# 24 token tiles transposed through DRAM and VectorE's 32x32 block transpose

## The chip, the core and the metric

The program runs on one core of a Trainium2 chip. Its engines work in parallel, each through its own list of instructions in order, and wait for each other by semaphores: TensorE (PE: matrix products and transposes; PEld: its weight loads), VectorE (DVE), ScalarE (ACT), GpSimd (POOL) and SyncE (SP), which here only issues transfers. SBUF has 128 partitions; PSUM takes the results of TensorE. The metric is the device time of one execution in microseconds, as the median of several runs.

## The reference

Two layers, each of FNet mixing and a linear attention block, on x of 2048 tokens by 640 columns, 32 heads of 20:

```
def _A_ref(x, dft_seq_re, dft_seq_im, dft_hid_re, dft_hid_im):
    a = jnp.einsum("bsd,ed->bse", x, dft_hid_re)
    b = jnp.einsum("bsd,ed->bse", x, dft_hid_im)
    return jnp.einsum("ts,bse->bte", dft_seq_re, a) - jnp.einsum("ts,bse->bte", dft_seq_im, b)

def _B_ref(x, wqkv, wo):
    qkv = (x @ wqkv).reshape(B, S, 3, H, Dh).transpose(2, 0, 3, 1, 4)
    q, k, v = qkv[0], qkv[1], qkv[2]
    phi = lambda t: jnp.where(t > 0, t + 1, jnp.exp(t)) + 1e-6
    pq, pk = phi(q), phi(k)
    kv = jnp.einsum("bhsd,bhse->bhde", pk, v)
    z = jnp.einsum("bhsd->bhd", pk)
    num = jnp.einsum("bhqd,bhde->bhqe", pq, kv)
    den = jnp.einsum("bhqd,bhd->bhq", pq, z)[..., None] + 1e-6
    return (num / den).transpose(0, 2, 1, 3).reshape(B, S, D) @ wo

for layer in range(2):
    x = x + _A_ref(_layernorm(x), dft_seq_re, dft_seq_im, dft_hid_re, dft_hid_im)
    x = x + _B_ref(_layernorm(x), wqkv, wo)
```

The change lies in `_B_ref`: in how the normalised x becomes an operand of the products for q and k.

## The kernel before

**Tiles and products.** The tokens lie in 16 tiles of 128 rows. A product of a tile with a 640x640 weight goes over five chunks of 128 columns of the tile, and each chunk must stand transposed in SBUF, its columns on the partitions. Single precision is made of two parts of a shorter type: hi, a rounded copy, and lo, the rest (`split`: the copy on ScalarE at L122, the subtraction at L123, on VectorE). `product` (L156) issues for each chunk hi·hi, hi·lo and lo·hi, each in two halves of 320 columns: 30 matmuls for a product.

**The first passes.** `keys_values` holds the place of the change. Its first loop (L282 on) runs over ten tiles, n = 0 to 9; a stage of Gram products (L244) follows, then the loop runs over the other six tiles, then a second Gram stage. That happens in both layers. An iteration for tile n does this, in the program's order:

- the statistics and the norm of tile n+1 (L116, x to t);
- the key product of tile n, and `phi` on its result: two steps from PSUM on ScalarE (L276, L277), an exp on ScalarE (L278), and one step on VectorE (L279), which gives s;
- POOL adds s to a running sum (L292);
- `chunks`: five transposes of tile n+1 on TensorE (L128) into PSUM, then hi from PSUM on ScalarE (L122) and lo, PSUM minus hi, on VectorE (L123);
- the query product of tile n, and the same `phi`, which gives pq;
- after some tiles, two further pieces of work. After tiles 4, 5, 8, 13 and 15 of the first layer SyncE saves two tiles of weights to DRAM (L199), from where the second layer loads them again. After the tiles 1, 2, 4, 5, 6, 7, 10, 11 and 12 in both layers there is a check: the program takes mirror symmetries of the DFT matrices for granted, and looks at them piece by piece on VectorE (L1071, L1088: ck, junk, cm), and falls back to a general path if they don't hold. Each check ends by issuing the loads of the next pieces (L1063) on SyncE, into the four buffers of the pool `raw`.

The transposes stand before the query product in TensorE's list, and the products of tile n+1 can start only with hi and lo.

**What sets the order.** A scheduler orders the instructions of TensorE, VectorE, ScalarE and POOL here, by priorities that follow the program's order, moved by a table of offsets (`AHEAD`, read by `ahead`), and by times of its own. SyncE keeps the program's order. Tiles come from pools: 12 buffers for the temporaries t (`tmp`), 31 for w and s (`wp`), 16 for pq, 4 for ck and raw weights, and four tiles of PSUM.

Of the kernel before, what the change touches and what calls it, by code (L numbers as in the profile page):

```python
# [8 lines left out]
F32 = mybir.dt.float32  # L9
# [5 lines left out]
S, D, H, DH = 2048, 640, 32, 20  # L15
NT = S // 128
ND = D // 128
# [17 lines left out]
SECOND = 'x02d x12d x22d x32d x00d x01d x10d x11d W00d W01d W02d W10d | w00a | w01a v00v W11d | w02a v01v W12d | v02v | R0a V0a w10a | O0p sfa v10v ffv dfp kfa r3p | w11a c2v v11v w12a nfa v12v nea t2p a3v b3v c3v V1a t3p p1v m1p u20v u21v u23v u24v u22v'  # L35
KM = (0, 0)
LEAD = 3
LOADS = (13, 13, 15, 15)
# [10 lines left out]
class K:  # L49
# [82 lines left out]

    def split_chunks(self, tp):
        hi, lo = self.temp(F32R), self.temp(F32R)
        self.split(tp[:, :D], hi, lo)
        return [[t[:, 128 * c : 128 * c + 128] for c in range(ND)] for t in (hi, lo)]
# [24 lines left out]
class Attention:  # L161
    def __init__(self, k, X, order, order2, wqkv, wo, mask, saved=None):
        self.k, self.X, self.order, self.order2, self.mask, self.saved = k, X, order, order2, mask, saved
        self.wqkv, self.wo, self.W = wqkv, wo, {}
        self.kept = {}

    def wt(self):
# [33 lines left out]
    def normed(self, n):  # L201
        xn = self.k.temp()
        x = self.X[self.order[n]]
        with self.k.ahead("stats", n):
            self.kept[n] = self.k.stats(
                x, xn if n in ASTATS[self.k.layer] else None, True, self.k.nc.vector if n in VSTATS[self.k.layer] else None
            )
        with self.k.ahead("norm", n):
            self.k.norm(x, xn, self.kept[n])
        return xn  # L210
# [45 lines left out]
    def keys_values(self, check=None, keep=1, saves=()):  # L256

        saves = list(saves)
        k, nc, W = self.k, self.k.nc, self.W
# [20 lines left out]

        x, acc, tail = self.x0, [], None
        for a, b in ((0, CUT), (CUT, NT)):  # L282
            pks = []
            for n in range(a, b):
                with k.ahead("normed", n + 1):
                    xn = self.normed(n + 1) if n + 1 < NT else None
                pk = self.slot()
# [5 lines left out]
                pks.append(pk)  # L293
                def chunks(xn=xn, n=n):
                    tp = k.transposed(xn)
                    with k.ahead("chunks", n):
                        return k.split_chunks(tp)
# [22 lines left out]
                if xn is not None:  # L320
                    x = got[0]
            G = [k.psum() for _ in range(3)]
            tail = tail or k.psum()
# [11 lines left out]
            if a == 0:  # L335
                acc = [self.slot() for _ in range(ND)]
# [8 lines left out]
        c = ND - 1  # L345
# [780 lines left out]
def fast_path(k, ctx, x, wqkv, wo, mask, sign, cls, cex, hid, ckc, ckh, out):  # L1126
# [6 lines left out]
    X = []  # L1133
    for i in range(NT):
        t = xp.tile([128, D], F32, name=f"x{i}")
# [54 lines left out]

    dram = ctx.enter_context(k.tc.tile_pool(name="dram", bufs=1, space=bass.MemoryType.DRAM))
    saved = {
# [3 lines left out]
    for layer in range(2):  # L1196
        att = Attention(k, X, order, list(range(NT)), wqkv, wo, mask, saved if layer else None)
        k.part = 2 * layer
        four.run(T, att)
        att.keys_values(check, saves=() if layer else [(*key, v) for key, v in saved.items()])  # L1200
        k.layer, k.part = 1, 2 * layer + 1
        T = Fold(k, X)
        if layer == 0:
            with k.tc.manual_schedule(engines=three):
                steps = T.script(SECOND, four)
                att.outputs_by_hand(T, steps)
                for _ in steps:
                    pass
        else:
            k.ends, flags = check.ends, []  # L1210
            att.outputs(store, lambda: flags or flags.append(verdict(k)))
# [174 lines left out]
```

## Time and profile before

| what | value |
| --- | --- |
| median of three runs | 768.3 us (767.63 to 768.64) |
| the profiled execution | 769.53 us, of which the span is 767.7 us |
| granted TensorE clock, mean of the span | 0.999 |
| first passes, layer 1: products L156 from, to | 79.0 to 172.9, and 217.0 to 268.3 us |
| first passes, layer 2: last product ends, and the second part | 540.0, and 583.9 to 635.1 us |
| Gram stages L244 between and behind them | 172.8 to 217.2, 268.1 to 296.6, 539.9 to 584.0, 634.9 to 663.2 us |
| TensorE busy, 66 to 165 us of the span | 97.83 of 99.00 us |
| TensorE busy, 165 to 240 us | 75.00 of 75.00 us |
| DMA share, 66 to 165 us | 0.44, at 133 GB/s |

The span runs from the first to the last instruction; the execution's own time is 1.8 us more. In the profile's rows the columns of the timeline are start, duration, engine, line, operation, the tile written and those read, and behind "<-" in brackets the idle time before it with what ended it. In the chain of waits a row has the start, the time, the engine, the tile and the line. A group's row has the busy time, the mean of one in ns, then the idle time before them and its releaser. In the view of one line or tile stand the least, the median and the highest duration in ns.

### The profile page before, as it was taken

The numbers are of one execution on the slowest core, as the hardware profiler recorded it, in microseconds if no ns is written. First come the engines' busy times: TensorE is split into PE (matmuls) and PEld (weight loads), VectorE is DVE, ScalarE is ACT, GpSimd is POOL, SyncE is SP. The second block draws the span as 40 slices with busy tenths as digits, with TensorE's granted clock in tenths as the row PEclk, the third lists the DMA queues.
The fourth block names the chain that finished last, engine by engine and source line by source line (L and its number), as shares of the span: only waits on it lengthen the run. The fifth ranks groups of instructions, "written<-read, shape, count | busy, mean of one in ns | idle before, by whom it ended". The sixth has DMA issues, their size and how long they took to land.

```text
span 767.7 us, 12873 instructions
## 1 busy us (share of the span) xinstructions
PE 742.9 (97%) x4884; PEld 706.1 (92%) x4884; DVE 572.8 (75%) x1152; ACT 340.5 (44%) x642; POOL 254.7 (33%) x267
## 2 busy tenths in 40 slices
PE   4899999999999999999999999999999999999996
PEld 1388999999999999899977999999999999989996
DVE  6998875767767585988974896576766867599982
ACT  7745444455334543455682234445432455331110
POOL 5237931220121111467762693111000111243300
PEclk9999999999999999999999999999999999999999
DMA  9322333653354641500052222254224404001112
GB/s 326 101 81 87 92 100 116 189 179 98 119 148 148 215 144 24 150 7 1 14 192 70 69 92 74 75 150 147 59 91 148 134 15 151 22 12 68 70 70 73
DMA packets 35102, 79.15 MB, mean 103 GB/s; under 512 B 4276, under 2 KB 6071, under 8 KB 35031
## 3 DMA queue, kind: packets, MB, share of 16 engines
q1 hardware_dynamic: 35031, 78.23, 32.1%
q8 instruction: 41, 0.67, 0.4%
q14 instruction: 30, 0.25, 0.1%
HBM read 66.01 MB, written 11.80 MB: 101 GB/s over the span
## 4 chain that ended last, share of the span: by engine, by line
PE 76%; DVE 12%; ACT 5%; POOL 2%; DMA 2%; issue 2%; SPq 1%; DVEq 0%; ACTq 0%; POOLq 0%
PE ps L156 47%; PE ps L244 17%; PE ps L128 3%; PE ps L1013 3%; PE ps L959 2%; PE ps L396 2%; PE ps L918 1%; DVE w L123 1%; DVE t L123 1%; ACT ab L779 1%; DMA x<-in_x 1%; DVE ps L458 1%; DVE x L484 1%; ACT ab L780 1%; DVE t L462 1%
## 5 line engine op out<-in xcount | busy, mean ns | idle before, releaser
L156 PE MATMUL ps<-w,t 128*128 128x320 f32 x2880 | 439.1, 311 | 0.5 <-DVE w L123 0.2
L156 PEld LDWEIGHTS ps<-w,t 128*128 128x128 f32 x2880 | 423.0, 188 | 1.6 <-DVE t L123 0.8
L292 POOL TENSOR_TENSOR t<-t,s 128x640 f32<-128x640 f32 x32 | 57.3, 1789 | 257.7 <-DVE s L279 250.1
L244 PE MATMUL ps<-t,t 128*128 128x256 f32 (+1 forms) x640 | 139.8, 309 | 0.0
L276 ACT ACTIVATE t<-ps 128x640 f32<-128x640 f32 x64 | 45.2, 706 | 154.2 <-PE ps L156 154.2
L244 PEld LDWEIGHTS ps<-t,t 128*128 128x128 f32 x640 | 107.3, 188 | 0.0
L1088 DVE CUSTOM_DVE_ANT_0 junk<-ck,ck 128x688 bf16<-128x688 f32 (+5 forms) x138 | 99.0, 718 | 6.1 <-DMA ck<-in_ck 4.2
L244 PE MATMUL ps<-w,t 128*128 128x384 f32 (+1 forms) x320 | 98.8, 310 | 0.3 <-DVE w L123 0.3
L442 POOL TENSOR_TENSOR t<-pq,t 128x640 f32<-128x640 f32 x32 | 53.7, 1684 | 95.9 <-ACT t L365 46.5
L122 ACT CAST t<-ps 128x640 fp32r<-128x640 f32 (+1 forms) x66 | 45.8, 695 | 78.9 <-PE ps L128 73.7
L123 DVE TENSOR_TENSOR t<-ps,t 128x640 fp32r<-128x640 f32 (+1 forms) x66 | 53.9, 818 | 26.5 <-ACT t L122 25.6
L279 DVE SCALAR_TENSOR_TENSOR pq<-t,pq 128x640 f32<-128x640 f32 x32 | 26.7, 835 | 52.2 <-ACT t L278 52.2
L244 PEld LDWEIGHTS ps<-w,t 128*128 128x128 f32 x320 | 60.1, 188 | 0.7 <-DVE w L123 0.5
L959 PE MATMUL ps<-t,u 128*128 128x322 f32 x306 | 48.8, 316 | 1.4 <-ACT t L986 0.7
L959 PEld LDWEIGHTS ps<-t,u 128*128 128x128 f32 x306 | 45.9, 189 | 3.2 <-issue 0.9
L278 ACT ACTIVATE t<-t 128x640 f32<-128x640 f32 x64 | 48.0, 751 | 0.0
L123 DVE TENSOR_TENSOR t<-t,t 128x640 fp32r<-128x640 f32 x32 | 27.8, 867 | 26.5 <-ACT t L122 26.1
L128 PE MATMUL ps<-ident,t 128*128 128x128 f32 x320 | 45.5, 273 | 1.0 <-DVE t L468 1.0
L116 DVE TENSOR_SCALAR t<-x,kept 128x640 f32<-128x640 f32 x60 | 43.4, 724 | 4.0 <-PE ps L244 4.0
L128 PEld LDWEIGHTS ps<-ident,t 128*128 128x128 f32 x320 | 38.3, 140 | 2.4 <-POOL t L442 1.0
L122 ACT CAST t<-t 128x640 fp32r<-128x640 f32 x32 | 23.3, 728 | 38.3 <-DVE t L116 33.6
L1013 PE MATMUL ps<-cw,ab 128*128 128x512 f32 x80 | 35.4, 596 | 2.0 <-ACT t L743 0.9
(180 smaller groups left out, 875.9 us busy)
## 6 DMA issues: line engine op xcount, KB each, us to landing
ck<-in_ck SPq DMA_DIRECT2D x48, 346.0 KB
ck<-in_ck SPq DMA_DIRECT2D x48, 344.0 KB
save<-w SPq DMA_DIRECT2D x20, 320.0 KB
w<-save SPq DMA_DIRECT2D x20, 320.0 KB
x<-in_x SPq DMA_DIRECT2D x16, 320.0 KB
out<-x SPq DMA_DIRECT2D x15, 320.0 KB
raw<-in_wqkv SPq DMA_DIRECT2D x10, 320.0 KB
s<-in_wqkv SPq DMA_DIRECT2D x10, 320.0 KB
```

The costliest lines, as they stand in the source:

```text
L122: self.nc.scalar.copy(hi, src)
L123: self.engine(pool).tensor_tensor(lo, src, hi.bitcast(F32), op=ALU.subtract)
L128: self.nc.tensor.transpose(tp[:, 128 * c : 128 * c + 128], src[:, 128 * c : 128 * c + 128], self.ident)
L156: nc.tensor.matmul(pu[:m, 512 * h : 512 * h + HD], s, w[:, HD * h : HD * h + HD], start=first, stop=last)
L244: nc.tensor.matmul(self.place(G, c, part), x[:, 128 * c : 128 * c + 128], p[:, f : f + n], start=start and i == 0, stop=stop and i == 2, s ...
L276: nc.scalar.activation(h2(e), halves(pu), AF.Relu, scale=-1.0)
L278: nc.scalar.activation(e, e, AF.Exp, scale=-1.0)
L292: nc.gpsimd.tensor_tensor(pksum, pksum, pk, op=ALU.add)
L442: k.nc.gpsimd.tensor_tensor(t1, self.PQ[self.order2[n]], self.zb, op=ALU.mult)
L959: self.k.nc.tensor.matmul(po[:, o : o + 322], s[:, f : f + 128], w[:, x, :], start=start, stop=stop)
L1013: self.k.nc.tensor.matmul(self.sum(j), T.out["o", q][:, 128 * j : 128 * j + 128], self.C[2, g], start=n == 0, stop=n == 3)
L1088: i = nc.vector.tensor_tensor_reduce(k.junk[:, : a.shape[1]], b, a, 1.0, 0.0, op0, op1, o)
```

## The change

Tiles 4 to 15 of each layer (`TURNED`), 24 in all, get their transposed chunks another way. The norm of such a tile is made three tiles ahead (`LEADS`) and stored by a transfer to a new tile in DRAM (`turn_out`, L139 of the changed kernel). Two tiles ahead a load brings it back (`turn_in`, L144), so that the four blocks of 160 columns come to lie on four groups of 32 partitions. VectorE's transpose of 32x32 blocks (`turned`, L148 and L149) then gives the chunks in SBUF; it writes every fourth column. hi and lo (L125, L126) are made from that tile, not from PSUM. Which column of x is on which partition of which chunk differs from before: the rows of the weights for q and k are put in that order on the host, and the tiles that TensorE still transposes (0 to 3) get it by their norm, which writes pieces of 32 columns (`chunked`). The general path keeps its old way.

```diff
@@ -34,6 +34,9 @@
...
 KM = (0, 0)
+TURNED = (tuple(range(4, 16)), tuple(range(4, 16)))
+TLOWS = ((), ())
+LEADS = (3, 2)
 LEAD = 3
 LOADS = (13, 13, 15, 15)
 ASTATS = ((11,), (1,))
@@ -130,9 +133,27 @@
             )
         return tp
 
-    def split_chunks(self, tp):
+    def turn_out(self, xn):
+
+        src = self.dram.tile([4, 128, D // 4], F32, name=self.nm("turn"))
+        self.nc.sync.dma_start(src.rearrange("a p c -> p a c"), xn.rearrange("p (a c) -> p a c", a=4))
+        return src
+
+    def turn_in(self, src):
+        z = self.temp()
+        self.nc.sync.dma_start(z, src.rearrange("a (j t) c -> (a j) (t c)", t=4))
+        return z
+
+    def turned(self, z, pool):
+        t = self.temp()
+        self.nc.vector.transpose(
+            t.rearrange("p (b j t) -> p t b j", b=ND, t=4), z.rearrange("p (t b i) -> p t b i", t=4, b=ND)
+        )
+        return self.split_chunks(t, pool)
+
+    def split_chunks(self, tp, pool=0):
         hi, lo = self.temp(F32R), self.temp(F32R)
-        self.split(tp[:, :D], hi, lo)
+        self.split(tp[:, :D], hi, lo, pool)
         return [[t[:, 128 * c : 128 * c + 128] for c in range(ND)] for t in (hi, lo)]
 
 
@@ -163,6 +184,7 @@
         self.k, self.X, self.order, self.order2, self.mask, self.saved = k, X, order, order2, mask, saved
         self.wqkv, self.wo, self.W = wqkv, wo, {}
         self.kept = {}
+        self.turns, self.tlows = (TURNED[k.layer], TLOWS[k.layer]) if saved is not None else ((), ())
 
     def wt(self):
         return self.k.wp.tile([128, 640], F32R, tag="w", name=self.k.nm("w"))
@@ -206,7 +228,11 @@
                 x, xn if n in ASTATS[self.k.layer] else None, True, self.k.nc.vector if n in VSTATS[self.k.layer] else None
             )
         with self.k.ahead("norm", n):
-            self.k.norm(x, xn, self.kept[n])
+            if n in self.turns:
+                self.k.norm(x, xn, self.kept[n])
+                return self.k.turn_out(xn)
+            chunked = xn.rearrange("p (b a i) -> p a b i", b=ND, a=4)
+            self.k.norm(x.rearrange("p (a b i) -> p a b i", a=4, b=ND), chunked, self.kept[n])
         return xn
 
     def begin(self):
@@ -278,12 +304,19 @@
             nc.scalar.activation(e, e, AF.Exp, scale=-1.0)
             nc.vector.scalar_tensor_tensor(out, e, 1e-6, out, op0=ALU.add, op1=ALU.add)
 
-        x, acc, tail = self.x0, [], None
+        x, acc, tail, out = self.x0, [], None, {}
         for a, b in ((0, CUT), (CUT, NT)):
             pks = []
             for n in range(a, b):
-                with k.ahead("normed", n + 1):
-                    xn = self.normed(n + 1) if n + 1 < NT else None
+                xn = None
+                for m in range(n + 1, n + 1 + LEADS[0]) if n == 0 else (n + 1, n + LEADS[0]):
+                    if m < NT and m not in out and (m == n + 1 or m in self.turns):
+                        with k.ahead("normed", m):
+                            out[m] = self.normed(m)
+                for m in range(n + 1, n + 1 + LEADS[1]) if n == 0 else (n + LEADS[1],):
+                    if m < NT and m in self.turns:
+                        out[m] = k.turn_in(out[m])
+                xn = out.get(n + 1)
                 pk = self.slot()
                 pu = proj(1, x)
                 with k.ahead("key", n):
@@ -292,6 +325,9 @@
                     nc.gpsimd.tensor_tensor(pksum, pksum, pk, op=ALU.add)
                 pks.append(pk)
                 def chunks(xn=xn, n=n):
+                    if n + 1 in self.turns:
+                        with k.ahead("chunks", n):
+                            return k.turned(xn, n + 1 in self.tlows)
                     tp = k.transposed(xn)
                     with k.ahead("chunks", n):
                         return k.split_chunks(tp)
@@ -1188,13 +1224,13 @@
     def store(i, a, b):
         nc.sync.dma_start(out[128 * i : 128 * i + 128, HD * a : HD * b], X[i][:, HD * a : HD * b])
 
-    dram = ctx.enter_context(k.tc.tile_pool(name="dram", bufs=1, space=bass.MemoryType.DRAM))
+    k.dram = dram = ctx.enter_context(k.tc.tile_pool(name="dram", bufs=1, space=bass.MemoryType.DRAM))
     saved = {
         (part, c): [dram.tile([128, D], F32, name=k.nm("save")) for _ in range(2)]
         for part in (1, 0) for c in range(ND)
     }
     for layer in range(2):
-        att = Attention(k, X, order, list(range(NT)), wqkv, wo, mask, saved if layer else None)
+        att = Attention(k, X, order, list(range(NT)), wqkv, wo, mask, saved if layer else {})
         k.part = 2 * layer
         four.run(T, att)
         att.keys_values(check, saves=() if layer else [(*key, v) for key, v in saved.items()])
@@ -1285,6 +1321,7 @@
     base, quad = quads()
     ps = quad.reshape(-1)
     pd = np.concatenate([np.arange(HC), np.arange(D - 1, HD, -1)])
+    turned = np.arange(D).reshape(4, ND, 32).transpose(1, 0, 2).reshape(-1)
     mask = as32(np.kron(np.eye(EC // DH, dtype=np.float32), np.ones((DH, DH), np.float32)))
     even = np.concatenate([quad[0, 0], quad[1, 0], quad[0, 1], quad[1, 1]])
     odd = np.concatenate([quad[2, 0], quad[3, 0], quad[2, 1], quad[3, 1]])
@@ -1350,7 +1387,7 @@
     ghid = lambda c: as32(c[pd][:, pd].T.reshape(ND, 128, D).transpose(1, 0, 2))
     ins = {
         "x": as32(A_x[0][ps][:, pd]),
-        "wqkv": as32(B_wqkv[pd]),
+        "wqkv": as32(np.concatenate([B_wqkv[pd][turned, : 2 * D], B_wqkv[pd][:, 2 * D :]], 1)),
         "wo": as32(B_wo[:, pd]),
         "mask": mask,
         "sign": as32(np.stack([2.0 * (np.arange(128) % 2) - 1.0, 1.0 - 2.0 * (np.arange(128) % 2)], 1).astype(np.float32)),
```

Where the order moves: VectorE, in an iteration with a check in the first layer. Here t_1465 is lo, s_1420 and pq_1468 are the results of `phi`, t_1521 is the norm of a later tile, and the rows with junk and cm are the check. Before:

```order
L1088 ISA junk,cm<-ck_1202,ck_1200 128x692
L1088 ISA cm 128x1
L1088 ISA junk,cm<-ck_1196,ck_1202 128x519
L1088 ISA cm 128x1
L123 TENSOR_TENSOR t_1465<-ps_1458,t_1464 128x640
L1088 ISA junk,cm<-ck_1196,ck_1202 128x173
L1088 ISA cm 128x1
L279 SCALAR_TENSOR_TENSOR s_1420<-t_1452,s_1420 128x640
L116 TENSOR_SCALAR t_1521<-x_128,kept_1522 128x640
L279 SCALAR_TENSOR_TENSOR pq_1468<-t_1500,pq_1468 128x640
```

The changed kernel at such a place; t_1448 is what the load brought, t_1599 its transpose, t_1602 lo, t_1656 the norm of the tile three ahead:

```order
L1124 ISA junk,cm<-ck_1432,ck_1434 128x692
L1124 ISA cm 128x1
L1124 ISA junk,cm<-ck_1434,ck_1428 128x519
L1124 ISA cm 128x1
L1124 ISA junk,cm<-ck_1434,ck_1428 128x173
L1124 ISA cm 128x1
L149 STREAM_TRANSPOSE t_1599<-t_1448 128x4x160
L305 SCALAR_TENSOR_TENSOR s_1561<-t_1593,s_1561 128x640
L126 TENSOR_TENSOR t_1602<-t_1599,t_1601 128x640
L119 TENSOR_SCALAR t_1656<-x_104,kept_1657 128x640
L305 SCALAR_TENSOR_TENSOR pq_1605<-t_1637,pq_1605 128x640
```

The block transpose stands behind the whole check and ahead of s; lo has moved from amid the check to behind s; the norm, still ahead of pq, is now of a tile two further on.

TensorE, from the end of one product to the next, before: the key product (ps_1532, weights w_675 and on), the transposes, then the query product (ps_1580, w_715 and on). t_1464 is hi, t_1465 lo.

```order
L156 MATMUL ps_1532<-w_699,t_1464 128x320 x2
L156 MATMUL ps_1532<-w_700,t_1464 128x320 x2
L156 MATMUL ps_1532<-w_699,t_1465 128x320 x2
L128 MATMUL ps_1569<-ident,t_1521 128x128 x5
L156 MATMUL ps_1580<-w_715,t_1464 128x320 x2
L156 MATMUL ps_1580<-w_716,t_1464 128x320 x2
```

In the changed kernel, where the query product of one tile (ps_1495) ends and the next tile (hi t_1490, lo t_1491) begins:

```order
L177 MATMUL ps_1495<-w_740,t_1379 128x320 x2
L177 MATMUL ps_1495<-w_739,t_1380 128x320 x2
L177 MATMUL ps_1562<-w_675,t_1490 128x320 x2
L177 MATMUL ps_1562<-w_676,t_1490 128x320 x2
L177 MATMUL ps_1606<-w_715,t_1490 128x320 x2
L177 MATMUL ps_1606<-w_716,t_1490 128x320 x2
L177 MATMUL ps_1562<-w_675,t_1491 128x320 x2
L177 MATMUL ps_1562<-w_681,t_1490 128x320 x2
```

The transposes are gone from between the products, and the first matmul that reads lo has four matmuls of the key product and four of the query product on hi ahead of it.

SyncE's list, an iteration with a check and a save, before; in_ck is the check's input:

```order
L199 DMA save_469<-w_676 128x640
L1063 DMA ck_1402<-in_ck 128x692
L1063 DMA ck_1404<-in_ck 128x692
L1063 DMA ck_1406<-in_ck 128x692
L1063 DMA ck_1408<-in_ck 128x692
L199 DMA save_470<-w_681 128x640
L199 DMA save_471<-w_682 128x640
```

In the changed kernel; turn_1335 was stored one tile earlier than turn_1446:

```order
L1099 DMA ck_1428<-in_ck 128x692
L1099 DMA ck_1430<-in_ck 128x692
L1099 DMA ck_1432<-in_ck 128x692
L1099 DMA ck_1434<-in_ck 128x692
L139 DMA turn_1446<-t_1436 128x4x160
L144 DMA t_1448<-turn_1335 128x640
L221 DMA save_470<-w_681 128x640
L221 DMA save_471<-w_682 128x640
```

A store and a load stand between the loads of the check and the saves of the next iteration.

## The prediction

> **What bounds the kernel now.** I read the page's busy shares first, then its chain of waits, then the table of windows for the first passes, which is where the change acts.
>
> ```profile
> PE 742.9 (97%) x4884; PEld 706.1 (92%) x4884; DVE 572.8 (75%) x1152; ACT 340.5 (44%) x642; POOL 254.7 (33%) x267
> PE 76%; DVE 12%; ACT 5%; POOL 2%; DMA 2%; issue 2%; SPq 1%; DVEq 0%; ACTq 0%; POOLq 0%
> ```
>
> TensorE is busy 97% of the span and holds 76% of the chain. An average doesn't say what one stage is worth, so I cut out iterations of the first pass: two of the first layer, then one of the second.
>
> ```profile
> core 0: us, PE busy (x) PEld busy (x) DVE busy (x) ACT busy (x) POOL busy (x), PEclk, DMA share, GB/s
> 149.85:159.20 9.35, 9.35 (x67) 9.35 (x67) 6.60 (x16) 4.44 (x8) 1.82 (x1) 1.00 0.48 152
> 159.20:168.55 9.35, 9.35 (x67) 9.34 (x67) 6.54 (x13) 5.69 (x10) 1.82 (x1) 1.00 0.88 283
> 607.61:616.96 9.35, 9.35 (x68) 9.35 (x67) 8.50 (x20) 4.45 (x8) 1.71 (x1) 1.00 0.50 152
> ```
>
> TensorE never idles there, at the full clock. VectorE has 2.75 us free of 9.35 in most iterations, but only 0.85 in the third row. The next rows, from the chain and from the timeline, say what the transposes cost TensorE.
>
> ```profile
> 149.85 8.80 PE ps L156 x60
> 159.20 8.80 PE ps L156 x60
> 158.49 0.71 PE L128 MATMUL ps<-ident,t 128*128 128x128 f32 x5
> ```
>
> One iteration is 60 products, 8.80 us on the chain, and five transposes. The period is 159.20 - 149.85 = 9.35, so a tile's transposes are worth 0.55 (their 0.71 overlaps the neighbours).
>
> **What goes.** Four tiles in each layer keep their transposes; 24 lose them: 24 x 0.55 = 13.2 us, the most that this can bring, if nothing else becomes late.
>
> **What is added on VectorE.** The built order moves the work of an iteration as shown above: the whole check now stands ahead of the block transpose, then s, then the low half, then the norm. I price this from one iteration with a check.
>
> ```profile
> 156.25 0.82 DVE L279 SCALAR_TENSOR_TENSOR pq<-t,pq 128x640 f32<-128x640 f32 x1 [2.64 <-ACT t L278]
> 156.99 0.33 DVE L1071 TENSOR_REDUCE ca<-ck 128x1 f32<-128x173 f32 x1
> ...
> 160.62 0.82 DVE L123 TENSOR_TENSOR t<-ps,t 128x640 fp32r<-128x640 f32 x1
> 161.36 0.33 DVE L1088 CUSTOM_DVE_ANT_0 junk<-ck,ck 128x173 bf16<-128x173 f32 x1
> ...
> 161.61 0.82 DVE L279 SCALAR_TENSOR_TENSOR s<-t,s 128x640 f32<-128x640 f32 x1
> 154.29 0.71 ACT L276 ACTIVATE t<-ps 128x640 f32<-128x640 f32 x1 [2.43 <-PE ps L156]
> 155.48 0.74 ACT L278 ACTIVATE t<-t 128x640 f32<-128x640 f32 x1
> 158.69 0.71 ACT L276 ACTIVATE t<-ps 128x640 f32<-128x640 f32 x1 [2.47 <-PE ps L156]
> 175.67 0.61 DVE L116 TENSOR_SCALAR t<-x,kept 128x640 f32<-128x640 f32 x1
> 176.37 0.73 ACT L122 CAST t<-t 128x640 fp32r<-128x640 f32 x1 [0.22 <-DVE t L116]
> ```
>
> Starts are 0.74 apart for the 0.82 us operations. The check takes 156.99 to 160.62 and 161.36 to 161.61, 3.88 us. pq stands idle for 2.64 us behind the norm until ScalarE's exp is done (155.48 + 0.74), and starts 0.03 later. A high half taken from SBUF starts 0.09 after VectorE's result (175.67 + 0.61 to 176.37) and takes 0.73.
>
> The block transpose itself is in no row. From below: the norm, also 128x640 with one input, 0.59 us. From above: half rate. A row of 320 columns takes 0.476, one of 640 takes 0.82, so 1.08 ns a column; two slots for each of 640 columns is 0.13 + 1.38 = 1.51 us.
>
> ```profile
> L116 DVE TENSOR_SCALAR t<-x,kept x60: 592/608/1858, 66.0 to 647.9; 128x640 f32<-128x640 f32 x60
> L96 DVE BATCH_NORM_STATS2 st<-x 128x6 f32<-128x320 f32 x30 | 14.1, 476 | 0.2 <-POOL x L991 0.2
> L123 DVE TENSOR_TENSOR u<-ps,u 128x512 fp32r<-128x512 f32 x12 | 8.0, 672 | 1.5 <-ACT u L122 1.5
> L942 DVE TENSOR_TENSOR u<-ps,u 128x512 fp32r<-128x512 f32 x10 | 6.6, 688 | 4.8 <-ACT u L941 4.5
> ```
>
> Its output goes to every fourth column. The two last rows are the nearest: L123 there writes every second column and takes no longer than L942, which writes them in a row. So I take the plain 0.82.
>
> Now the deadlines, counted from ScalarE's first step on a query product (154.29). pq starts 1.96 later, the check at 2.70, the block transpose at 6.58, done at 7.40; with 0.09, 0.73 and 0.03 the high half is there at 8.25. TensorE wants it after 60 products, 8.80, less the 0.20 by which ScalarE trails TensorE (158.49 to 158.69): 8.60, so 0.35 is to spare. The low half ends at 9.1; the new TensorE order runs four key and four query products on the high half first, so it isn't wanted before 8.60 + 8 x 0.147 = 9.77. Without a check the transpose runs 3.9 us earlier. Nothing is late.
>
> VectorE's own loop is closer. The low half now reads two SBUF tiles, and POOL's sum (L292) starts 0.14 us after s.
>
> ```profile
> 638.35 0.82 DVE L279 SCALAR_TENSOR_TENSOR s<-t,s 128x640 f32<-128x640 f32 x1
> 639.09 0.82 DVE L123 TENSOR_TENSOR w<-s,t 128x640 fp32r<-128x640 f32 x1
> 639.31 2.01 POOL L292 TENSOR_TENSOR t<-t,s 128x640 f32<-128x640 f32 x1 [8.10 <-DVE s L279]
> 639.82 2.18 DVE L123 TENSOR_TENSOR t<-t,t 128x640 fp32r<-128x640 f32 x1
> 601.82 1.71 POOL L292 TENSOR_TENSOR t<-t,s 128x640 f32<-128x640 f32 x1 [7.96 <-DVE s L279]
> 602.02 1.86 DVE L116 TENSOR_SCALAR t<-x,kept 128x640 f32<-128x640 f32 x1
> L123 DVE TENSOR_TENSOR t<-ps,t x66: 770/820/826, 72.9 to 753.8; 128x640 fp32r<-128x640 f32 x64, 40x640 fp32r<-40x640 f32 x2
> L123 DVE TENSOR_TENSOR t<-t,t x32: 817/826/2183, 165.6 to 650.7; 128x640 fp32r<-128x640 f32 x32
> ```
>
> Here an operation that starts behind s keeps its 0.82 and POOL waits; the next one with two SBUF inputs then stands until POOL is done (2.18). The norm does too, 1.86. With one input in PSUM, as the low half has before, none of 66 exceeds 0.83. In the new order the low half follows s, and the norm pays: it ends 0.35 after POOL (603.88 against 603.53), POOL 2.15 after s. The loop of a check iteration is then pq 0.74, check 3.88, transpose 0.74, s 0.82, and 2.43 to the next free slot (2.15 + 0.36 - 0.08): 8.61, under 8.80. The spare 0.19 is the cover: a transpose above 1.0 us ends it.
>
> In two iterations of the second layer the check has two pieces (the third row of windows).
>
> ```profile
> 596.05 0.51 DVE L1071 TENSOR_REDUCE ca<-ck 128x1 f32<-128x344 f32 x1
> 600.85 0.82 DVE L279 SCALAR_TENSOR_TENSOR s<-t,s 128x640 f32<-128x640 f32 x1
> ```
>
> From 596.05 to the norm at 602.02, less the low half and s within it (0.74 each), is 4.49. The loop is 9.22, so each loses 0.42: 0.85 together.
>
> **What is added elsewhere.** The high half from SBUF costs ScalarE 0.03 more a tile, at 44% busy: nothing, since the next query's first step comes later. The norms of the other eight tiles write pieces of 32 columns: nothing while they have the idle 2.64 ahead of pq. 48 more DMAs stand on SP's queue; behind them wait the loads of the checks and the saves of weights.
>
> ```profile
> 159.07 3.46 SPq L1063 DMA_DIRECT2D ck<-in_ck  x4
> 162.58 2.75 SPq L199 DMA_DIRECT2D save<-w  x4
> 5.63 7.17 DMA x<-in_x
> 68.99 5.00 DMA raw<-in_wqkv
> ck<-in_ck SPq DMA_DIRECT2D x48, 346.0 KB
> save<-w SPq DMA_DIRECT2D x20, 320.0 KB
> ```
>
> The four check loads go out as the check frees their buffers; then the store, whose norm was long done; then a load of an earlier store. At about 0.4 us an issue this load leaves 1.3 us after a check ends. Its transpose has its turn right after the next check, 8.80 later: 7.5 us to land. Loads of 320 KB, the size of this one, land in 5.00, and in 7.17 where all of x is under way. So it is hidden, without much room. The price if not is below.
>
> **Sum.** 13.2 - 0.85 = 12.3 us. The profiled execution took 769.5 (span 767.7) and would take 757.2; the runs' median is 768.3, 1.2 lower, and goes to **756.0**.
>
> **Rivals.** (1) *The block transpose runs at half rate*, 1.51. Then the loop of a check iteration is 9.29, against 9.35 before: only the 8 tiles without a check gain in full (4.4), the 14 with a single check gain 0.06 each (0.8), the two double ones take 9.91, 0.56 more than before (-1.1). About 4.1 us: 764.2. For it: every write lands 16 bytes from the last; against it: no stride of 8 bytes cost anything. [...]
>
> (2) *The low half loses SBUF to POOL.* In a check iteration it starts 0.85 us after the transpose ends (0.09 + 0.73 + 0.03), POOL at 0.88 (s ends at 0.82 - 0.08, and 0.14): a margin of 0.03. A loss costs 2.18 - 0.82 = 1.36, and TensorE's stall gives the next iteration that much room, so every second of 16 pays: 10.9. 766.9, no measurable change. [...]
>
> (3) *Slower: the load through DRAM lands late* and holds VectorE's queue at the transpose, with s, the low half, the norm and pq behind it, so TensorE waits for the next tile. Price: landing time less 7.5, in every second of 16 iterations (the stall gives the next load its time). A gain of 12.3 is used up at 9.0 us. For it: in 159.20 to 168.55 the queues already run at 0.88, and an iteration with check (4 x 346 KB), two saves (2 x 320) and a turned tile (its store and load, 2 x 320) moves 2.66 MB, 9.4 us at that row's 283 GB/s. 1.9 x 8 = 15: 771. Against it: the load stands ahead of its iteration's saves, and most iterations have none.
>
> **Chances.** The forecast 62%, with 754.5 to 758.5 as its own range (0.55 a tile kept, up to 0.15 lost in each check iteration); half rate 17%; POOL first 7%; late load 14%. A range of 754.0 to 767.0 leaves out the late load and little else. A difference under 0.2% (1.5 us) can't be told from none. Faster by more: the first two and a little of the third, 80%; within: 6%; slower: 14%.
>
> **What would show it.** A period of 8.80 between key products in the first passes, with no idle time of TensorE behind the low or high half, shows the main term. A mean near 0.82 for the transpose shows its price; 1.5 and a period near 9.3 beside checks show rival 1. Low halves of 2.2 us show rival 2. Idle time of VectorE ended by a DMA ahead of the block transpose shows rival 3. The forecast is wrong if the transpose takes over 1.0 us, or if the second passes or the later stages, which I take as unmoved, lengthen.

## The result and the profile after

The changed kernel takes 769.5 us (median of 8 runs, 768.82 to 770.67), the kernel before 768.2 beside it (8 runs, 767.62 to 769.59): a ratio of 1.0018, interval 1.0007 to 1.0029. The predicted time was 756.0. TensorE's transposes are gone as planned, 120 fewer, and nothing came of it. One of the four timed runs of e11_all, below, took 916.4 us at a mean granted clock of 0.753; its median and ratio are those of the other three. The page of the changed kernel, busy shares and chain:

```profile
PE 736.0 (96%) x4764; PEld 694.4 (90%) x4764; DVE 628.5 (82%) x1176; ACT 341.8 (45%) x642; POOL 261.7 (34%) x267
PE 51%; DVE 28%; ACT 8%; issue 6%; POOL 3%; DMA 3%; SPq 0%; DVEq 0%; POOLq 0%; ACTq 0%
```

TensorE's share of the chain fell from 76% to 51%, VectorE's rose from 12% to 28%, and VectorE is busy 55.7 us longer. Three iterations of the first passes, in the columns of the windows before; the cuts lie at ScalarE's first steps on query products, the first two in the first layer, the third in the second:

```profile
133.23:142.53 9.30, 9.06 (x60) 8.80 (x60) 9.15 (x16) 4.48 (x7) 2.28 (x1) 1.00 0.90 290
142.53:151.96 9.43, 9.07 (x60) 8.81 (x60) 9.14 (x16) 4.48 (x9) 2.27 (x1) 1.00 0.73 223
611.71:620.96 9.25, 9.11 (x62) 9.11 (x63) 8.06 (x19) 4.46 (x9) 2.75 (x2) 1.00 0.52 168
```

The period is 9.30 and 9.43 us where 9.35 stood before and 8.80 was forecast. VectorE is busy 9.15 of 9.30. One iteration with a check, from the timeline:

```profile
126.34 0.82 DVE L305 SCALAR_TENSOR_TENSOR pq<-t,pq 128x640 f32<-128x640 f32 x1 [0.47 <-ACT t L304]
127.08 0.32 DVE L1107 TENSOR_REDUCE ca<-ck 128x1 f32<-128x173 f32 x1
...
131.09 1.34 DVE L149 STREAM_TRANSPOSE t<-t 128x640 f32<-128x640 f32 x1
132.28 0.81 DVE L305 SCALAR_TENSOR_TENSOR s<-t,s 128x640 f32<-128x640 f32 x1
132.46 0.73 ACT L125 CAST t<-t 128x640 fp32r<-128x640 f32 x1 [1.17 <-DVE t L149]
133.22 0.83 DVE L126 TENSOR_TENSOR t<-t,t 128x640 fp32r<-128x640 f32 x1
133.23 2.29 POOL L325 TENSOR_TENSOR t<-t,s 128x640 f32<-128x640 f32 x1 [7.71 <-DVE s L305]
133.97 1.90 DVE L119 TENSOR_SCALAR t<-x,kept 128x640 f32<-128x640 f32 x1
135.78 0.81 DVE L305 SCALAR_TENSOR_TENSOR pq<-t,pq 128x640 f32<-128x640 f32 x1
```

Read it as a loop without a gap: pq 0.74, the check 4.01 (127.08 to 131.09), the block transpose 1.19 to the next start, s 0.94, the low half 0.75, the norm 1.81: 135.78 - 126.34 = 9.44. The high half (132.46) can start only behind the block transpose, so it ends at 133.19, and TensorE waits for it. What TensorE and VectorE waited for, from the table of waits (us in total, times, longest):

```profile
PEld ps L177 <- ACT t L125: 10.1, 15, 2.0
PEld ps L177 <- DVE t L126: 4.6, 6, 1.1
PE ps L177 <- ACT t L125: 5.8, 9, 1.8
PE ps L177 <- DVE t L126: 3.0, 6, 0.8
DVE t L149 <- DMA t<-turn: 6.0, 3, 2.1
```

The first four are the high and the low half. The gaps of over 0.28 us between the starts of neighbouring matmuls in the first passes, each less the usual 0.147 (8.80 us for 60), come to 11.2 us of stalls (before: 0.3).

One place costs most, at the end of the first pass of the first layer:

```profile
156.64 2.38 POOL L106 TENSOR_TENSOR kept<-ve,mhalf 128x1 f32<-128x1 f32 x3
158.37 0.61 DVE L115 TENSOR_SCALAR t<-x,kept 128x640 f32<-128x640 f32 x1 [0.96 <-POOL kept L106]
...
162.87 1.58 POOL L325 TENSOR_TENSOR t<-t,s 128x640 f32<-128x640 f32 x1 [2.67 <-DVE s L305]
162.93 2.21 DVE L126 TENSOR_TENSOR t<-t,t 128x640 fp32r<-128x640 f32 x1
162.95 1.44 PE L177 MATMUL ps<-w,t 128*128 128x320 f32 x8 [1.77 <-ACT t L125]
...
165.19 9.30 PE L177 MATMUL ps<-w,t 128*128 128x320 f32 x52 [0.81 <-DVE t L126]
```

The norm of tile 11 stands amid the check here and waits 0.96 us for POOL; the block transpose is late by that; the low half starts 0.06 behind POOL's sum and takes 2.21. TensorE stands for 1.77 and 0.81 us, and its next 52 matmuls take 9.30 us, where 52 x 0.147 is 7.64. The windows show why:

```profile
165.20:168.00 2.80, 2.80 (x10) 2.80 (x11) 2.32 (x4) 1.35 (x2) 0.00 (x0) 0.50 1.06 391
168.00:171.00 3.00, 3.00 (x21) 3.00 (x21) 2.29 (x3) 0.28 (x1) 0.00 (x0) 0.94 0.82 234
```

The granted clock was 0.50 at first: ten matmuls started 0.267 us after the one before and one 0.43, which is 1.5 us more than at 0.147. The rest of the row's surplus is the last matmul's own length (the 2880 of L177 take 0.31 us in the mean).

### The profile page after: what moved, and what is told of

The parts are those of the page before. It is cut to its first block, busy times and chain, and to the rows that moved or that the text cites. A ratio compares the mean times of both kernels' runs of the same rounds, so it can differ in the third digit from the quotient of the medians.

```text
span 767.6 us, 12773 instructions
## 1 busy us (share of the span) xinstructions
PE 736.0 (96%) x4764; PEld 694.4 (90%) x4764; DVE 628.5 (82%) x1176; ACT 341.8 (45%) x642; POOL 261.7 (34%) x267
## 4 chain that ended last, share of the span: by engine, by line
PE 51%; DVE 28%; ACT 8%; issue 6%; POOL 3%; DMA 3%; SPq 0%; DVEq 0%; POOLq 0%; ACTq 0%
PE ps L177 24%; PE ps L270 16%; DVE junk L1124 6%; PE ps L1049 4%; PE ps L995 3%; DVE t L126 3%; DVE t L149 2%; DVE t L119 2%; DVE w L126 2%; ACT t L125 2%; PE ps L131 1%; PE ps L954 1%; DVE pq L305 1%; DMA ck<-in_ck 1%; DVE st L99 1%
## 5 line engine op out<-in xcount | busy, mean ns | idle before, releaser
L177 PE MATMUL ps<-w,t 128*128 128x320 f32 x2880 | 438.9, 311 | 8.8 <-ACT t L125 5.8
L177 PEld LDWEIGHTS ps<-w,t 128*128 128x128 f32 x2880 | 424.1, 189 | 14.5 <-ACT t L125 10.1
L325 POOL TENSOR_TENSOR t<-t,s 128x640 f32<-128x640 f32 x32 | 64.6, 2018 | 284.7 <-DVE s L305 284.7
L302 ACT ACTIVATE t<-ps 128x640 f32<-128x640 f32 x64 | 45.1, 705 | 125.1 <-PE ps L177 119.5
L126 DVE TENSOR_TENSOR t<-t,t 128x640 fp32r<-128x640 f32 x56 | 50.2, 896 | 26.9 <-PE ps L270 16.1
L125 ACT CAST t<-t 128x640 fp32r<-128x640 f32 x56 | 40.8, 728 | 53.6 <-DVE t L119 26.5
L125 ACT CAST t<-ps 128x640 fp32r<-128x640 f32 (+1 forms) x42 | 28.9, 691 | 78.9 <-PE ps L131 77.9
L119 DVE TENSOR_SCALAR t<-x,kept 128x640 f32<-128x640 f32 x60 | 62.7, 1050 | 0.6 <-DMA turn<-t 0.6
L126 DVE TENSOR_TENSOR t<-ps,t 128x640 fp32r<-128x640 f32 (+1 forms) x42 | 34.1, 815 | 5.8 <-ACT t L125 4.8
L305 DVE SCALAR_TENSOR_TENSOR pq<-t,pq 128x640 f32<-128x640 f32 x32 | 27.2, 852 | 13.3 <-ACT t L304 13.3
L149 DVE STREAM_TRANSPOSE t<-t 128x640 f32<-128x640 f32 x24 | 32.1, 1339 | 6.0 <-DMA t<-turn 6.0
L125 ACT CAST t<-s 128x640 fp32r<-128x640 f32 x32 | 23.2, 725 | 29.4 <-PE ps L270 29.4
```

Of the source, the lines that this page charges most:

```text
L119: self.nc.vector.tensor_scalar(out, x, m, rs, op0=ALU.subtract, op1=ALU.mult)
L125: self.nc.scalar.copy(hi, src)
L126: self.engine(pool).tensor_tensor(lo, src, hi.bitcast(F32), op=ALU.subtract)
L149: self.nc.vector.transpose(t.rearrange("p (b j t) -> p t b j", b=ND, t=4), z.rearrange("p (t b i) -> p t b i", t=4, b=ND))
L177: nc.tensor.matmul(pu[:m, 512 * h : 512 * h + HD], s, w[:, HD * h : HD * h + HD], start=first, stop=last)
L325: nc.gpsimd.tensor_tensor(pksum, pksum, pk, op=ALU.add)
```

## Experiments

**Theory 1**: VectorE became the bound beside a check. Its loop of 9.44 us took the gain; the two large terms are the block transpose at 1.34 and the norm behind POOL's sum at 1.9. **Theory 2**: the loads through DRAM are late, or their traffic is in the way. A second question is what makes the block transpose 1.34.

The table compares the kernels by what their profiled runs spent in the first passes: from ScalarE's first step on the first key product to its first step on the last product ahead of the Gram stage, in each of the four parts, summed. "Rest" is the profiled execution's time less that sum. The median is that of the timed runs, the ratio that of their time to the kernel before, as its 95% interval.

| kernel | first layer | second layer | sum | rest | median | ratio |
| --- | --- | --- | --- | --- | --- | --- |
| before | 89.2 + 46.7 | 89.5 + 46.7 | 272.1 | 497.4 | 768.3 | |
| changed | 91.7 + 45.1 | 88.5 + 47.3 | 272.7 | 496.8 | 769.5 | 1.0007 to 1.0029 |
| e1_dense | 87.8 + 44.0 | 86.2 + 46.0 | 264.0 | 495.9 | 760.5 | 0.9878 to 0.9911 |
| e2_nosum | 88.0 + 44.6 | 87.0 + 45.6 | 265.2 | 494.1 | 759.2 | 0.9856 to 0.9889 |
| e3_free | 88.0 + 46.2 | 88.4 + 46.2 | 268.8 | 498.1 | 768.2 | 0.9973 to 1.0003 |
| e5_pair | 86.7 + 44.0 | 86.2 + 46.1 | 263.1 | 498.2 | 761.8 | 0.9903 to 0.9941 |
| e6_latesum | 90.3 + 45.1 | 88.3 + 46.9 | 270.6 | 497.4 | 768.9 | 0.9992 to 1.0013 |
| e8_pairstat | 86.6 + 44.1 | 86.8 + 46.1 | 263.6 | 497.3 | 761.5 | 0.9890 to 0.9934 |
| e9_latesum2 | 88.1 + 44.7 | 87.8 + 45.9 | 266.5 | 517.8 | 784.2 | 1.0184 to 1.0223 |
| e11_all | 85.9 + 44.0 | 86.5 + 44.5 | 260.9 | 520.2 | 781.0 | 1.0142 to 1.0193 |
| c1_nosum | 89.2 + 46.7 | 89.4 + 46.7 | 272.1 | 493.8 | 766.6 | 0.9965 to 0.9987 |
| c2_traffic | 89.3 + 46.9 | 89.4 + 46.7 | 272.3 | 497.5 | 769.4 | 1.0001 to 1.0020 |
| e12_more | 88.4 + 44.0 | 88.0 + 46.0 | 266.5 | 499.5 | 766.4 | 0.9966 to 0.9987 |

### e1_dense: the block transpose writes its runs side by side

```diff
-            t.rearrange("p (b j t) -> p t b j", b=ND, t=4), z.rearrange(...)
+            t.rearrange("p (b t j) -> p t b j", b=ND, t=4), z.rearrange(...)
```

> The block transpose writes its 32-column runs side by side instead of to every fourth column; nothing else moves (the tokens of a turned tile then stand in another order in its chunks). Theory 1 (the 1.34 us of the block transpose come from the writes 16 bytes apart): it falls to about 0.82, VectorE's loop beside a check falls from 9.44 to about 8.95, and the 14 or so iterations with a check gain about 0.5 each: 762 to 764. Theory 2 (1.34 is what the operation costs in any layout): it stays at 1.34 and the time at 769.5.

760.5 us, 9.0 below the changed kernel and 1.5 below the range expected, with one access pattern changed. It leaves the tokens of a turned tile in another order, so it only measures. The block transposes of the changed kernel, then of this one (least, median and highest ns):

```profile
L149 DVE STREAM_TRANSPOSE t<-t x24: 1309/1340/1352, 113.1 to 624.3; 128x640 f32<-128x640 f32 x24
```

```profile
L149 DVE STREAM_TRANSPOSE t<-t x24: 833/840/845, 112.1 to 615.1; 128x640 f32<-128x640 f32 x24
```

0.84 in place of 1.34: the 0.5 us are the price of the layout, not of the operation. A loop of this kernel beside a check, from its timeline:

```profile
129.70 0.84 DVE L149 STREAM_TRANSPOSE t<-t 128x640 f32<-128x640 f32 x1
130.46 0.78 DVE L305 SCALAR_TENSOR_TENSOR s<-t,s 128x640 f32<-128x640 f32 x1
131.34 0.83 DVE L126 TENSOR_TENSOR t<-t,t 128x640 fp32r<-128x640 f32 x1
132.08 1.88 DVE L119 TENSOR_SCALAR t<-x,kept 128x640 f32<-128x640 f32 x1
133.88 0.81 DVE L305 SCALAR_TENSOR_TENSOR pq<-t,pq 128x640 f32<-128x640 f32 x1
...
138.62 0.84 DVE L149 STREAM_TRANSPOSE t<-t 128x640 f32<-128x640 f32 x1
```

138.62 - 129.70 = 8.92. Beside the other single checks there are no stalls left; 2.3 us stay near 160, 1.75 at the three iterations with several checks of the second layer's second part, 0.5 early in the second layer.

### e2_nosum: POOL's running sum left out for the turned tiles

```diff
-                    nc.gpsimd.tensor_tensor(pksum, pksum, pk, op=ALU.add)
+                    n in self.turns or nc.gpsimd.tensor_tensor(pksum, pksum, pk, op=ALU.add)
```

> POOL's running sum of the keys is left out for the turned tiles (so the denominators are not those of the reference). Theory 1 (VectorE's own loop beside a check, 9.44 us against 8.80 of TensorE, took the gain, and 1.26 of it is the norm that stands behind POOL's sum): the norm falls from 1.86 to 0.61, the loop to about 8.2, TensorE's stalls of 0.3 to 1.1 us in the first passes go (8.2 of 11.4 us), 757 to 762. Theory 2 (the loads through DRAM arrive late): the sum has nothing to do with them, VectorE still waits 6.0 us for them, 768 to 770.

759.2. The group of the norms on the page, of the changed kernel and then of this one; this one's wait for the loads; and a loop from its timeline:

```profile
L119 DVE TENSOR_SCALAR t<-x,kept 128x640 f32<-128x640 f32 x60 | 62.7, 1050 | 0.6 <-DMA turn<-t 0.6
```

```profile
L119 DVE TENSOR_SCALAR t<-x,kept 128x640 f32<-128x640 f32 x60 | 42.6, 715 | 3.0 <-DMA turn<-t 3.0
```

```profile
DVE t L149 <- DMA t<-turn: 6.8, 3, 2.4
```

```profile
125.90 0.83 DVE L305 SCALAR_TENSOR_TENSOR pq<-t,pq 128x640 f32<-128x640 f32 x1 [1.73 <-ACT t L304]
...
130.66 1.34 DVE L149 STREAM_TRANSPOSE t<-t 128x640 f32<-128x640 f32 x1
...
133.53 0.61 DVE L119 TENSOR_SCALAR t<-x,kept 128x640 f32<-128x640 f32 x1
134.75 0.82 DVE L305 SCALAR_TENSOR_TENSOR pq<-t,pq 128x640 f32<-128x640 f32 x1 [0.61 <-ACT t L304]
```

The mean norm falls from 1.05 us to 0.72; VectorE has idle time again (0.61) although its block transpose still takes 1.34. VectorE's wait for the loads is as long as before (6.8 against 6.0) and the time fell nonetheless: theory 2 falls for the loads.

### c1_nosum and c2_traffic: the controls, on the kernel before

c1_nosum leaves out the same sums; c2_traffic stores the same tiles, loads 22 of the 24 and uses nothing of it:

```diff
+                if xn is not None and n > 2 and self.saved is not None:
+                    out = k.dram.tile([4, 128, D // 4], F32, name=k.nm("turn"))
+                    nc.sync.dma_start(out.rearrange("a p c -> p a c"), xn.rearrange("p (a c) -> p a c", a=4))
+                    outs.append(out)
+                    if n > 3:
+                        nc.sync.dma_start(k.temp(), outs[-2].rearrange("a (j t) c -> (a j) (t c)", t=4))
```

> The kernel before, with POOL's running sum left out for the same 24 tiles as in e2_nosum (so the denominators are not those of the reference). Theory: the kernel before waits for TensorE in its first passes and the sum is hidden there, so nothing is gained in them; the Gram stages may lose some 0.7 us each as in e2_nosum: 766.5 to 768.5. If the sum itself costs what e2_nosum won (10 us), it would be near 758, and e2_nosum would say nothing of the block transpose.

> The kernel before, and for each of the same tiles its store to DRAM and a load one tile later that nothing reads (22 loads of 24); TensorE still transposes. Theory: 15 MB more of traffic beside 100 GB/s cost nothing in the first passes, 767.5 to 769.5. Rival: the traffic itself delays the checks' loads, the saves or the reloads of weights, and is what e5_pair lacks to the 756 forecast: 771 or more.

c1: 766.6, and its first passes take 272.1 as before; what it gains lies in the rest (493.8 against 497.4). So the 7.5 us that e2_nosum gained in the first passes (272.7 to 265.2) exist only where VectorE is the bound; the 2.7 that it gained in the rest have their like here. c2: first passes 272.3, and a ratio of 1.0011: the traffic costs the first passes nothing that shows, and the whole some 0.8 us.

### e3_free: only tiles 5, 10 and 15 turned

```diff
-TURNED = (tuple(range(4, 16)), tuple(range(4, 16)))
+TURNED = ((5, 10, 15), (5, 10, 15))
```

> Only tiles 5, 10 and 15 of each layer are turned, those whose block transpose has no check ahead of it; 6 tiles in place of 24. Theory 1: each still gains its 0.55 us, 3.3 in all: 764.5 to 765.5, with no TensorE stall in the first passes. Theory 2 (DRAM traffic and late loads eat the gain wherever a tile is turned): a gain under 1 us, 767.5 to 768.5.

The first passes of the profiled run take 268.8, 3.3 less than before: 0.55 for each tile, as expected. The median does not show it: 768.2, from ten runs spread over 766.07 to 770.54, lies in the range that theory 2 gave. Part of that goes with the granted clock: the four runs with a mean of 0.998 or 0.999 took 766.1 to 766.9, and eleven such runs of the kernel before 767.9 to 768.6, 1.7 more by the medians. The gain in place is measured in one run; what the runs lost elsewhere stays open.

### e5_pair: every second column, with the tokens in their order

Each tile is stored by two transfers, rows 0 to 63 and 64 to 127, so that the block transpose writes 8 bytes apart:

```diff
-        self.nc.sync.dma_start(src.rearrange("a p c -> p a c"), xn.rearrange("p (a c) -> p a c", a=4))
+        for u in range(2): self.nc.sync.dma_start(src[u].rearrange("a q c -> q a c"), xn[64 * u : 64 * u + 64].rearrange("q (a c) -> q a c", a=4))
...
-            t.rearrange("p (b j t) -> p t b j", b=ND, t=4), z.rearrange("p (t b i) -> p t b i", t=4, b=ND)
+            t.rearrange("p (b u j t) -> p u t b j", b=ND, u=2, t=2), z.rearrange("p (u t b i) -> p u t b i", u=2, t=2, b=ND)
```

> All is computed: each turned tile is stored by two transfers in an order of rows by which the block transpose writes every second column, 8 bytes apart, two writes in each 16 bytes. Theory 1 (the price comes with a step of 16 bytes from write to write): 0.84 us as with side by side, 759.5 to 761.5. Rival (any step costs, in proportion): about 1.0 us, VectorE's loop 9.1 beside a check, 763 to 766. If the third transfer of a tile delays SyncE's queue: 1 to 3 us above 760.5 with VectorE idle behind the loads.

```profile
L149 DVE STREAM_TRANSPOSE t<-t x24: 834/841/848, 113.1 to 616.4; 128x640 f32<-128x640 f32 x24
```

0.84 at 8 bytes as at 4; 1.34 at 16. 761.8 us, 0.992 of the kernel before (0.9903 to 0.9941): it computes everything and is faster than both kernels. The third transfer of a tile shows no price in the first passes: 263.1 against 264.0 for e1_dense, and VectorE's wait for the loads, at the block transpose, comes to 6.6 us (8.4 there). The median is 1.3 above e1_dense and 0.3 above the range expected, and that lies in the rest (498.2 against 495.9); its cause is open.

### e8_pairstat: e5_pair with the statistics of tile 11 on VectorE

```diff
-ASTATS = ((11,), (1,))
+ASTATS = ((), (1,))
```

> e5_pair with the statistics of tile 11 of the first layer on VectorE rather than ScalarE, so that the norm of tile 11 no longer stands amid a check and waits for POOL. Theory: TensorE's stalls of 1.30 and 1.03 us near 160 us (the low half that started 0.01 us behind POOL's sum and took 2.26) go: 2 to 2.5 us below e5_pair, 757.5 to 759. Rival: the place is late for another reason (the saves' and checks' transfers at 0.86 of the DMA engines): as e5_pair.

A miss. The expectation took the stalls near 160 from e1_dense (1.30 and 1.03); e5_pair has one of 1.25. It is gone, but 1.0 us of others appeared at 96 and 115, so the pass took 86.6 (86.7 in e5_pair), and 761.5 is within the spread of e5_pair.

### e6_latesum, e9_latesum2, e11_all: the sum in the Gram stages

e6_latesum issues the sum in the Gram loop. e9_latesum2 starts it with the last key of the pass, which no sum can then precede, and takes the total one tile before the end of the second Gram stage; e11_all adds that to e8_pairstat. The core of e9_latesum2:

```diff
-                with k.ahead("pks", n):
-                    nc.gpsimd.tensor_tensor(pksum, pksum, pk, op=ALU.add)
...
+            for pk in pks[::-1]: nc.gpsimd.tensor_tensor(pksum, pks[-2] if pk is pks[-1] and not a else pksum, pk, op=ALU.add) if a or pk is not pks[-2] else None
```

> The changed kernel with POOL's running sum moved out of the first passes into the Gram stages behind them, where VectorE is less busy; all is computed. Theory 1: the first passes do as without the sum (TensorE stalls down by about 8 us) and the Gram stages hide the sum, 757 to 762. Rival: the sum meets VectorE's low halves in the Gram stages (2.2 of 4.4 us a tile are busy there, more beside a check) and gives 2 to 6 us back, 763 to 768.

A miss of the edit: the scheduler put each sum where its key was ready, in the first passes as before, and 768.9 is no difference. It still gave one thing. It has the stalls near 160 of the changed kernel, and yet, in its windows:

```profile
165.20:168.00 2.80, 2.80 (x19) 2.80 (x20) 2.07 (x4) 1.35 (x2) 0.00 (x0) 1.00 1.05 384
```

Full clock, 19 matmuls where the changed kernel got 10, and a part of 90.3 us where that took 91.7, after the same stalls, from its timeline:

```profile
162.88 1.45 PE L177 MATMUL ps<-w,t 128*128 128x320 f32 x8 [1.77 <-ACT t L125]
165.11 1.14 PE L177 MATMUL ps<-w,t 128*128 128x320 f32 x6 [0.79 <-DVE t L126]
```

> The changed kernel, its block transpose at 1.34 us, with POOL's running sum made to start from the last key of a pass, so that it can't run before the Gram stage; all is computed. Theory 1: the first passes do as in e2_nosum (norm 0.61, VectorE's loop 8.2), 759 to 762, if the Gram stages (44.6 and 28.4 us) stay as they are. Rival: there the sum meets the low halves, some 1.3 us each for the 9 and 6 sums, of which TensorE feels a part: 762 to 768.

> e8_pairstat and the late sum of e9_latesum2 together. If VectorE's loop beside a check is what is left, it falls to about 7.7 us, the double checks of the second layer fit too, and TensorE runs at 8.80 a tile: 755 to 757.5. Rival: e8_pairstat has no stall left worth 1 us except at the double checks, and the late sum gives back what it brings: within 1 us of e8_pairstat.

Both are slower, and say two things. In the first passes theory 1 holds: e11_all, with the cheap transpose and without the sum, takes 260.9 there, 11.2 below the kernel before, with two stalls left (1.04 and 0.42 us). In the Gram stages, which wait for VectorE's operations as well, the sums cost more than that, and both times lie far above what was expected of them. e9_latesum2, timeline:

```profile
175.14 11.35 POOL L360 TENSOR_TENSOR t<-t,s 128x640 f32<-128x640 f32 x6
175.66 1.82 DVE L119 TENSOR_SCALAR t<-x,kept 128x640 f32<-128x640 f32 x1
177.40 2.16 DVE L126 TENSOR_TENSOR w<-s,t 128x640 fp32r<-128x640 f32 x1
...
179.49 2.17 DVE L126 TENSOR_TENSOR t<-t,t 128x640 fp32r<-128x640 f32 x1
179.62 0.69 PE L270 MATMUL ps<-w,t 128*128 128x384 f32 x1 [4.60 <-DVE w L126]
```

In the unbroken row of six sums two norms take 1.82 and 1.84 us, where the shortest norm of this run takes 0.59, and two low halves 2.16 and 2.17; TensorE stands for 4.60 and then runs at a lower clock (0.78 in the mean from 180 to 190 us). The rest grew from 496.8 to 517.8.

### e12_more: e5_pair with tile 3 turned too

```diff
-TURNED = (tuple(range(4, 16)), tuple(range(4, 16)))
+TURNED = (tuple(range(3, 16)), tuple(range(3, 16)))
```

> e5_pair with tile 3 turned as well, 26 tiles; all is computed. It stands behind a check; with the block transpose at 0.84 such an iteration still gains: 2 x 0.55 = 1.1 us below e5_pair, 760 to 761.3. Rival: its store and load come too close to the start of the pass, VectorE waits for the load: as e5_pair or above.

The rival's time held, 766.4, but not for the late load that it named. Stalls of 0.3, 0.6 and 0.9 us came up between 88 and 108 us. A norm there waits for a store to free its tile, and a piece of the check that takes 0.88 elsewhere takes 2.01 while POOL's sum runs:

```profile
89.60 2.63 DVE L119 TENSOR_SCALAR t<-x,kept 128x640 f32<-128x640 f32 x2 [1.03 <-DMA turn<-t]
...
100.08 2.54 POOL L325 TENSOR_TENSOR t<-t,s 128x640 f32<-128x640 f32 x1 [2.09 <-DVE s L305]
...
101.35 2.01 DVE L1124 CUSTOM_DVE_ANT_0 junk<-ck,ck 128x692 bf16<-128x692 f32 x1
```

Near 160 us 2.3 are lost, as in e1_dense. The second layer's first part takes 88.0, 1.8 more than in e5_pair, but all of that lies in its last step, for which ScalarE waited 2.68 us until a store had freed a tile; up to the step before, the two parts take 82.4 and 82.5:

```profile
536.01 0.70 ACT L302 ACTIVATE t<-ps 128x640 f32<-128x640 f32 x1 [2.68 <-DMA turn<-t]
```

## Why the prediction was wrong

**The main term was right.** 0.55 us a tile is what a transpose costs TensorE: e3_free took 3.3 us out of the first passes with 6 tiles, and e11_all, without VectorE's limit, 11.2 of 13.2, with 1.5 us of stalls left.

**The step that failed: "So I take the plain 0.82."** The block transpose takes 1.34. The bounds, 0.59 and 1.51, held it, but the choice between them went by two rows with writes 8 bytes apart, and this operation writes 16 bytes apart. e5_pair shows that those rows told the truth about 8 bytes (0.84); they said nothing of 16. With 0.84 in place of 1.34 (e1_dense) the time is 760.5, so this step is worth 9.0 of the 13.5 us by which 756.0 was missed. Rival 1 alone gave the 16 bytes a price. Its half rate, two slots a column, was an estimate, and no run shows it: here the operation takes 1.6 times as long (1.34 against 0.84). I weighed rows that didn't have the disputed property above the one argument that named it.

**The cover was too thin, as was said, and thinner than that.** "A transpose above 1.0 us ends it" was right in kind. But the loop came to 9.44, not to 8.61 + 0.45 = 9.06 (1.19 to the next start, where 0.74 was taken). e1_dense has the same gap with the transpose at 0.84: 8.92 against 8.61. The check took 4.01 to the next operation (3.88 taken), the low half starts 0.88 behind s because it waits for ScalarE's high half (0.82 taken), and from there to pq it is 2.54 (2.43 taken). The wait for the high half I had counted for TensorE's deadline, but not in VectorE's loop, where it stands again.

**Rival 1** thus named the right property at 17%, with a price too high (1.51) and a time too low (764.2): it left the loop at 9.29 and let two iterations with double checks lose 0.56 each, where there were three and TensorE stood 0.9 to 1.1 us behind each, in the third because the low half lost to POOL.

**Rival 2** was no general loss: the low half kept its 0.83 at most places (median of 56: 0.825). It did happen near 160 and near 620 us (2.21 and 2.12), where other work had moved the two starts against each other; near 620 a piece of the check stood between s and the low half:

```profile
620.45 1.71 POOL L325 TENSOR_TENSOR t<-t,s 128x640 f32<-128x640 f32 x1 [6.37 <-DVE s L305]
620.73 2.12 DVE L126 TENSOR_TENSOR t<-t,t 128x640 fp32r<-128x640 f32 x1
```

A change too small to measure, for which the chances had 6%, did come, but not by this rival's road.

**Rival 3** fell. VectorE's 6.0 us of waiting for loads lie in three iterations without a check (1.94, 2.06 and 2.05), where it has the time: no stall of TensorE follows there.

**What no step had**: the lower clock behind the stalls near 160 us (0.50 from 165.20 to 168.00), 1.5 us, and the norm of tile 11 that the scheduler put amid a check. The sum nearly closes in the first passes: the transposes were worth 13.2 us, and a loss of 0.6 was measured (272.1 to 272.7), so 13.8 went elsewhere, of which 0.85 was forecast. The gaps of 0.25 us and more between matmuls, each less 0.147 and with the 1.5 of lower clock among them, come to 13.7, against 0.4 before: 13.3.

## What to carry to other kernels

Work that is moved to an engine with "room" has to be laid into that engine's loop at its tightest iteration, with every wait of the loop in it, before the gain is counted; an average busy share of 75% hid an iteration with 0.19 us to spare by the forecast's count and none by e1_dense's (8.92 against 8.80). Price an operation by a row that shares the property in dispute (here the step between writes), and where there is none, take the range's costly end seriously. A layout whose writes lie 8 bytes apart in place of 16 (0.84 us against 1.34) cost one more transfer a tile and turned a change that gained nothing into one that gains 6.4 us (768.2 to 761.8).

## What the runs showed of the hardware

The block transpose of 128x640 fp32 takes 0.84 us with writes 4 or 8 bytes apart and 1.34 us with 16 (medians of 24 in e1_dense, e5_pair and the changed kernel).

Where a low half with both inputs in SBUF met POOL's sum in the first passes of the changed kernel, the one that started first kept its time, and the edge is fine: a low half that started 0.01 us ahead of the sum kept 0.83 and POOL took 2.29 in place of 1.58; one that started 0.06 behind took 2.21. It isn't so for every operation of VectorE: the pq of e12_more at 100.37 us, 0.29 behind the sum at 100.08, kept 0.82, and POOL took 2.54:

```profile
100.37 0.82 DVE L305 SCALAR_TENSOR_TENSOR pq<-t,pq 128x640 f32<-128x640 f32 x1
```

TensorE's clock: after stalls of 1.77 and 0.81 us with eight matmuls between them the changed kernel ran at 0.50 from 165.20 to 168.00 us and at 0.94 from there to 171.00, and e6_latesum, with 1.77 and 0.79 at the same place, ran at 1.00 in both windows. All eight timed runs of the changed kernel have a mean clock of 0.996 or 0.997, as the profiled one has with this stretch in it, and of the ten of e6_latesum three have 0.998 and seven less. But of 19 runs of the kernel before, timed beside e3_free, eight have no more than 0.997 too, and where a run without a trace lost its clock isn't known. So behind 2.6 us of standing in all the changed kernel lost another 1.5 us to the clock, and e6_latesum did not; that the stalls are the cause is argued from where the low clock lies, and not shown.
